# An attention and MoE kernel on one core: one weight quarter ahead of batch 1's tokens, and batch 1's transposes and state products moved in between the pieces of batch 0's second product

## The chip, the cores and the metric

The kernel runs on one core of one Trainium2 chip. The metric is the device time in microseconds (us), the median of three runs: 219.97 us before the change (219.83 to 220.05).

## The reference, cut to what matters

```python
# x: 8 batches, 8 heads, 512 tokens, 64;  state: 8, 8, 32, 64
scores  = x @ state^T / 8                 # softmax over the 32 states
xread   = softmax(scores)  @ state
scores2 = state @ x^T / 8                 # softmax over the 512 tokens
sread   = softmax(scores2) @ x
y = concatenate([xread, sread], axis=2)   # 544 rows per batch, 8 heads x 64 = 512 columns
h = y @ w_in                              # 512 x 2048
out = maximum(0.01 * h, h) @ w_out        # 2048 x 512
```

Inputs and output are fp32; the kernel computes in bf16 with fp32 sums.

## The kernel before, in words

**Algebra.** For the 512 token rows of a batch, xread @ w_in is never formed as such. The kernel multiplies the state by w_in first: M = state @ w_in, of 256 x 2048, held as two halves g of 128 rows (`a_m`, L322, in four column chunks c of 512; `m_evict`, L342, copies a chunk from PSUM to the tile M). FF1 is then `aT` (the probabilities, transposed) times M: per 128 columns j of the 2048, two matmuls (g = 0, 1) and one leaky relu on ACT into hT (`ff1`, L352; for batch 0 `ff1_0`, L570, and `relu0`, L577, two j at a time). FF2 is hT times w_out: for each of the four token tiles i, sixteen matmuls of 128 x 512, cut into four pieces jq of four matmuls (`piece`, L377). A piece with jq = 0 opens a PSUM bank for its tile, the one with jq = 3 copies it out and stores it. The state rows go through FF1 and FF2 at the end.

**Names used below.** PE is TensorE, DVE VectorE, ACT ScalarE, POOL GpSimd, SP SyncE. `VEC`, `SCA` and `POO` are copies on DVE, ACT and POOL. (b, c) behind M is batch and chunk. The softmax of a batch is `a_scores` (L209, PE, into the PSUM tile sc), `a_shift` (L260, DVE: row maxima mrow, spread mrowb, difference sh), `a_exp` (L264, ACT), `a_probs` (L267, DVE: sums, reciprocals, spread, product: aT). The second softmax is `a_max2` (L271, DVE, ends with mcols), `a_exp2` (L277, ACT, once per g, reads sc), `a_probs2` and `a_a2t` (DVE, and a transposed DMA on SP), and `a_sread` (PE).

**Order of work.** The schedule is manual: each engine runs its instructions in the order in which the code issues them, and waits in place for what an instruction needs. DMA queues too are in the order of issue: SP's, ACT's and POOL's. POOL issues all of w_in (four chunks), the tokens of batch 1, all of w_out (four quarters `load_w_out(c)`, c serves the pieces jq = c) and the tokens of batch 2. The tokens go to a buffer xl and are cast to bf16 (xb, `cast_x`, L102); batch 1's are transposed on PE (`a_xt_pe`, L190), 16 transposes in two PSUM banks, each copied to xT. The state of batches 2 to 7 is loaded by eight DMAs on SP (`load_state`, L162), cast by POOL and transposed by a DMA (`state_t`, L170): scores and M of batch 2 need it (st_t).

**PSUM.** There are eight banks: two of each of the tags ph and py, two in the one buffer "sc", two in the one buffer "big". A new tile of a tag waits until the last reader of the tile that had its bank is through.

**Around the change, before it.** Batch 0's tokens are cast in three steps (L518 to L522). Batch 0's FF1 (L584 to L605) ends with j = 14; in its loop, at j = 8, stand M(0,3), the scores of batch 0 and the cast of batch 1's tokens on DVE and POOL, and at j = 12 M(1,1). Then (L607 to L640) come exp2 of batch 0, the transposes of batch 1, pieces 0 and 1 of jq = 0, the scores of batch 1 with M(1,2), pieces 2 and 3 (in banks of ph), the loads of the state, exp and exp2 of batch 1, a_probs, the cast of batch 2's tokens on ACT, the pieces of jq = 1 and 2, jq = 3 for tiles 2 and 3, state_t. The loop at L648 is FF1 of batch 1 (s = 0 to 15), with the two last pieces of batch 0 and the first ones of batch 1 in between; at s = 2 are the transposes of batch 2, at s = 4 its scores, M(1,3) and M(2,0), at s = 8 its exp, at s = 10 and 11 its exp2, at s = 13 M(2,1) and M(2,2). The loop at L683 does batches 2 to 7.

Of the kernel before, what the change touches and what calls it, by code (L numbers as in the profile page):

```python
# [9 lines left out]
P = 128  # L10
B, H, S, D = 8, 8, 512, 64
NS = 32
DFF = 2048
DM = 512
SROW = S + NS
NT = S // P
# [4 lines left out]
FP32 = mybir.dt.float32  # L21
# [6 lines left out]
def kernel(  # L28
# [9 lines left out]
    nc = tc.nc  # L38
# [8 lines left out]
    psum = ctx.enter_context(tc.tile_pool(name="psum", bufs=2, space=bass.MemoryType.PSUM))  # L47
# [5 lines left out]
    VEC, SCA, POO = nc.vector.tensor_copy, nc.scalar.copy, nc.gpsimd.tensor_copy  # L53
# [38 lines left out]
    w_out_bf = wpool.tile([P, 16, DM], BF16, name="w_out_bf")  # L92
    xs, xl = {}, {}

    def load_x(b, eng):
        xl[b] = xpool.tile([P, H, NT * D], FP32, name="xl", tag="xl", bufs=2)
        eng.dma_start(xl[b][:], x[b].rearrange("h (p t) d -> p h (t d)", t=NT))

    def open_xb(b):
        xs[b] = xpool.tile([P, NT, H, D], BF16, name="xb", tag="xb")  # L100

    def cast_x(b, h0, h1, copy):  # L102
        copy(  # L103
            xs[b][:, :, h0:h1].rearrange("p t h d -> p h t d"),
            xl[b][:, h0:h1].rearrange("p h (t d) -> p h t d", t=NT),
        )

    def cast_x0(h0, h1, copy):
        u = h0 // NK
        copy(  # L110
            xs[0][:, :, h0:h1].rearrange("p t h d -> p h t d"),
            xf[u][:, h0 - NK * u:h1 - NK * u].rearrange("p h (t d) -> p h t d", t=NT),
        )

    def load_w_in(c):
        nc.gpsimd.dma_start(
            w_in_bf[:, :, DM * c:DM * (c + 1)],
            moe_w_in[:, DM * c:DM * (c + 1)].rearrange("(k p) f -> p k f", p=P),
        )

    def load_w_out(c):
        nc.gpsimd.dma_start(
            w_out_bf[:, 4 * c:4 * (c + 1), :],
            moe_w_out[DM * c:DM * (c + 1), :].rearrange("(j p) f -> p j f", p=P),
        )
# [33 lines left out]
    stf = consts.tile([P, B - 2, P], FP32, name="stf")  # L159
    stb = consts.tile([P, B - 2, P], BF16, name="stb")  # L160

    def load_state():  # L162
        for k in range(NK):
            for g in range(2):
                nc.sync.dma_start(
                    stf[NS * k:NS * (k + 1), :, D * g:D * (g + 1)],
                    state[2:, 2 * k + g].rearrange("b n d -> n b d"),
                )

    def state_t():  # L170
        POO(stb[:], stf[:])
        nc.sync.dma_start_transpose(st_t[:], stb[:].rearrange("p b q -> p (b q)"))
# [94 lines left out]
    def a_probs(a):  # L267
        a.aT = att.tile([P, 2, S], BF16, name="aT", tag="aT")
        block_probs(a.aT[:], a.e1, NB)
# [52 lines left out]
    def a_m(a, c, tag):  # L322
        if c == 0:
            a.M = mpool.tile([P, 2, DFF], BF16, name="M", tag="M")
        if tag in ("ph", "py", "phpy"):
            pm = [psum.tile([P, DM], FP32, name="pm", tag=t) for t in (tag[:2], tag[-2:])]
            at = [t[:] for t in pm]
        else:
            pm = psum.tile([P, 2, DM], FP32, name="pm", tag=tag, bufs=1)
            at = [pm[:, g, :] for g in range(2)]  # L330
        for k in range(NK):
            for g in range(2):
                v, r = (k // 2, 2 * (k % 2) + (g ^ (k // 2))) if a.b == 0 else (g, k)
                nc.tensor.matmul(  # L334
                    at[v][NS * r:NS * (r + 1)],
                    lhsT=st_of(a, g, k),
                    rhs=w_in_bf[D * g:D * (g + 1), k, DM * c:DM * (c + 1)],
                    start=True, stop=True,
                )
        return pm  # L340

    def m_evict(a, c, pm, copy):  # L342
        cols = slice(DM * c, DM * (c + 1))
        if isinstance(pm, list):
            for g in range(2):
                copy(a.M[:, g, cols], pm[g][:])  # L346
        else:
            copy(a.M[:, :, cols], pm[:])  # L348
# [25 lines left out]

    ys = {}

    def piece(b, hT, i, jq, tag="py", copy=SCA):  # L377
        if jq == 0:
            y = ys[b, i] = Y()
            y.py = psum.tile([P, DM], FP32, name="py", tag=tag)  # L380
        y = ys[b, i]
        for j in range(4 * jq, 4 * jq + 4):
            nc.tensor.matmul(  # L383
                y.py[:], lhsT=hT[:, j, P * i:P * (i + 1)], rhs=w_out_bf[:, j, :],
                start=(j == 0), stop=(j == 15),
            )
        if jq == 3:
            ysb = ypool.tile([P, DM], FP32, name="ysb", tag="ysb")
            copy(ysb[:], y.py[:])  # L389
            if b == B:  # L390
                for bb in range(4):
                    r0 = (4 * i + bb) * SROW + S
                    nc.sync.dma_start(out[r0:r0 + NS, :], ysb[NS * bb:NS * (bb + 1), :])
            else:
                nc.sync.dma_start(rows_of(b)[i], ysb[:])

    def rows_of(b):
        return out[b * SROW:b * SROW + S, :].rearrange("(p t) f -> t p f", t=NT)
# [20 lines left out]
    a0, a1, a2 = att_of[:3]  # L419
# [99 lines left out]
    cast_x0(2, 4, SCA)  # L519
    pxt = x0_half(0)  # L520
    xt0_evict(0, pxt, (VEC, SCA))
    cast_x0(4, 8, VEC)  # L522
    for c in range(2, 4):
        load_w_in(c)
    load_x(1, nc.gpsimd)
    for c in range(4):
        load_w_out(c)
    load_x(2, nc.gpsimd)
    a0.aT = att.tile([P, 2, S], BF16, name="aT", tag="aT")
# [18 lines left out]
    pm = a_m(a0, 0, "sc")  # L548
# [12 lines left out]
    h0 = hpool.tile([P, 16, S], BF16, name="hT", tag="hT")  # L561
# [5 lines left out]
        ph = [psum.tile([P, S], FP32, name="ph", tag=tag) for _ in range(2)]  # L567
        return ph, [p[:] for p in ph]

    def ff1_0(banks, j, g):  # L570
        for v in range(2):
            nc.tensor.matmul(  # L572
                banks[v], lhsT=a0.M[:, g, P * (j + v):P * (j + v + 1)], rhs=a0.aT[:, g, :],
                start=(g == 0), stop=(g == 1),
            )
# [7 lines left out]

    t0, b0 = open_ff1_0("py")  # L584
    t2, b2 = open_ff1_0("sc")
    for g in range(2):
        ff1_0(b0, 0, g)
        ff1_0(b2, 2, g)
    relu0(t0, 0)
    relu0(t2, 2)  # L590
    m_evict(a0, 2, a_m(a0, 2, "big"), VEC)
# [1 line left out]
    for j, tag in ((4, "py"), (6, "sc"), (8, "py"), (10, "ph"), (12, "py"), (14, "ph")):  # L593
        t, bk = open_ff1_0(tag)
        for g in range(2):
            ff1_0(bk, j, g)
        relu0(t, j)
        if j == 8:
            m_evict(a0, 3, a_m(a0, 3, "big"), VEC)
            a_scores(a0)  # L600
            a_max2(a0)
            cast_x(1, 0, 4, VEC)
            cast_x(1, 4, 8, POO)
        elif j == 12:
            m_evict(a1, 1, a_m(a1, 1, "big"), VEC)  # L605

    tags = ("py", "py", "ph", "ph")  # L607
    for g in range(2):
        a_exp2(a0, g)
    for t0 in (0, 2):  # L610
        ps = psum.tile([P, 2, NK, P], BF16, name="pxt2", tag="ph")
        a_xt_pe(a1, ps, t0, t0 + 2)
        VEC(a1.xT[:, t0:t0 + 2], ps[:])
    for i in (0, 1):
        piece(0, h0, i, 0, tags[i])
    a_scores(a1)
    m_evict(a1, 2, a_m(a1, 2, "big"), SCA)
    a_shift(a1)
    a_max2(a1)
    for i in (2, 3):  # L620
        piece(0, h0, i, 0, tags[i])
    nc.vector.memset(stf[:, 0, D - 1:D + 1], 0.0)
    load_state()
    a_exp(a1)
    for g in range(2):
        a_exp2(a1, g)
    a_probs(a1)
    open_xb(2)
    cast_x(2, 0, 8, SCA)
    for jq in (1, 2):  # L630
        for i in range(NT):
            piece(0, h0, i, jq, tags[i])
    for i in (2, 3):
        piece(0, h0, i, 3, tags[i], VEC if i % 2 else SCA)
    state_t()
    a_probs2(a0)
    a_a2t(a0)
    a_probs2(a1)
# [9 lines left out]
    for s in range(16):  # L648
        ff1(a1, h1, s)
        if s % 2:  # L650
            pb, hT, i, jq = fill[s // 2]
            piece(pb, hT, i, jq, copy=VEC if s == 3 else SCA)
        if s == 2:
            a_xt_full(a2)
            VEC(a2.xT[:], a2.pxt[:])
        elif s == 4:
            a_scores(a2)
            pm = a_m(a1, 3, "big"), a_m(a2, 0, "phpy")
            m_evict(a1, 3, pm[0], SCA)
            m_evict(a2, 0, pm[1], VEC)  # L660
            a_shift(a2)
            a_max2(a2)
            cast_x(3, 0, 8, POO)
        elif s == 8:
            a_exp(a2)
        elif s == 9:
            a_sread(a0)
        elif s in (10, 11):
            a_exp2(a2, s - 10)
            if s == 11:  # L670
                a_probs(a2)
                a_probs2(a2)
        elif s == 13:
            pm = [a_m(a2, 1, "big"), a_m(a2, 2, "sc")]
            m_evict(a2, 1, pm[0], VEC)
            m_evict(a2, 2, pm[1], SCA)
            a_open(att_of[3], 3)
            a_xt_dma(att_of[3])
# [4 lines left out]
    for b in range(2, B):  # L683
        hT = hpool.tile([P, 16, S], BF16, name="hT", tag="hT")
# [5 lines left out]
        for s in range(16):  # L690
# [38 lines left out]
            pb, i, jq = order[s]  # L729
# [6 lines left out]
    b = B - 1  # L736
# [43 lines left out]
```

## Time and profile before

| | |
|---|---|
| median of three runs | 219.97 us (219.83 to 220.05) |
| the profiled execution | 220.79 us |
| its span, first to last instruction | 218.7 us |
| PE busy | 210.1 us (96%) |
| ACT busy | 136.6 us (62%) |
| DVE busy | 102.9 us (47%) |
| POOL busy | 21.6 us (10%) |
| granted clock of PE | 1.00 |
| PE's share of the chain that ended last | 87% |

Times in the profile are microseconds from the start of the span. A row of the timeline gives start, duration, engine, line, operation, tiles and count, and in brackets the idle time of that engine just before, with what ended it. A row of the stretches gives the stretch, its length, and for PE, PE's weight loads, DVE, ACT and POOL the busy time with the number of instructions, then the granted clock, the DMA engines' share and GB/s. A matmul of 128 x 512 is shown as 0.379 us long, but the next one starts 0.216 us after it: matmuls overlap.

### The profile page before, as it was taken

To read this page: it belongs to the slowest core of one execution; us is meant where nothing else is said; L and a number is where in the kernel's file an instruction comes from. 1 tells how busy PE (TensorE), PEld (TensorE's weight loads), DVE (VectorE), ACT (ScalarE), POOL (GpSimd) and SP (SyncE) were. 2 spreads that over 40 slices of the span, in tenths; PEclk is the share of its full clock that TensorE was granted. 3 is DMA by queue.
4 is the path that set the end of the run, shared out by engine and by line. 5 is a ranking of instruction groups with operands and counts; after the bars stand their busy time and mean duration, and the time that the engine had idled before them with its cause. 6 is when DMAs were issued, how large, how long until landed. Compare 5 with 4: busy or idle time off the path is not lost.

```text
span 218.7 us, 3729 instructions
## 1 busy us (share of the span) xinstructions
PE 210.1 (96%) x1524; PEld 99.0 (45%) x1524; DVE 102.9 (47%) x155; ACT 136.6 (62%) x255; POOL 21.6 (10%) x35
## 2 busy tenths in 40 slices
PE   7999999996999999999999999999999999999994
PEld 2543444452345444444444444444444445466553
DVE  1768696699678408660767056724673000000000
ACT  3459646568869647964787477847685665554420
POOL 8811001003030003000300030000000000000000
PEclk9999999999999999999999999999999999999999
DMA  6999993986941493149313950271114111111123
GB/s 183 221 218 284 205 262 100 158 226 167 251 126 48 112 251 119 51 108 251 121 51 76 254 148 34 66 148 51 48 48 99 48 48 48 51 47 49 48 51 96
DMA packets 37632, 27.17 MB, mean 124 GB/s; under 512 B 22256, under 2 KB 32880, under 8 KB 37616
## 3 DMA queue, kind: packets, MB, share of 16 engines
q1 hardware_dynamic: 32704, 20.52, 36.0%
q0 software_dynamic: 4768, 6.29, 14.2%
q10 hardware_dynamic: 144, 0.13, 0.5%
q8 instruction: 12, 0.20, 0.4%
q14 instruction: 4, 0.03, 0.1%
HBM read 17.30 MB, written 8.91 MB: 120 GB/s over the span
## 4 chain that ended last, share of the span: by engine, by line
PE 87%; DVE 5%; DMA 3%; ACT 2%; SPq 1%; issue 1%; ACTq 0%
PE py L383 50%; PE ph L355 20%; PE pm L334 4%; PE ph L366 3%; PE pspin L130 2%; PE ph L572 2%; DMA st_t<-stb 2%; PE psr L307 1%; PE sc L213 1%; DVE mcols L275 1%; PE php L572 1%; DMA out_dram<-ysb 1%; DVE M L346 1%; DVE mrowb L231 1%; DVE M L348 1%; DVE sh L233 1%
## 5 line engine op out<-in xcount | busy, mean ns | idle before, releaser
L383 PE MATMUL py<-w_out_bf,hT 128*128 128x512 bf16 x496 | 125.5, 379 | 0.0
L360 ACT ACTIVATE hT<-ph 128x512 bf16<-128x512 f32 x112 | 67.0, 601 | 42.6 <-PE ph L355 42.6
L383 PEld LDWEIGHTS <-hT 128*128 128x128 bf16 x496 | 47.0, 98 | 57.4 <-issue 4.9
L355 PE MATMUL ph<-aT,M 128*128 128x512 bf16 x224 | 66.1, 379 | 2.2 <-ACT hT L360 1.9
L355 PEld LDWEIGHTS <-M 128*128 128x128 bf16 x224 | 21.6, 98 | 29.1 <-issue 3.9
L389 ACT COPY ysb<-py 128x512 f32<-128x512 f32 x31 | 18.2, 586 | 11.5 <-PE py L383 11.5
L223 DVE TRANSPOSE_TENSOR_REDUCE mrow<-sc 128x32 f32<-128x1024 f32 x7 | 8.7, 1249 | 32.1 <-PE sc L213 32.1
L411 DVE COPY ysh<-pyh 128x256 f32<-128x256 f32 x1 | 0.4, 425 | 47.7 <-PE pyh L406 47.7
L103 POOL CAST xb<-xl 128x2048 bf16<-128x2048 f32 (+1 forms) x6 | 10.5, 1751 | 89.1 <-DMA xl<-in_x_dram 69.9
L348 ACT CAST M<-pm 128x1024 bf16<-128x1024 f32 x14 | 14.2, 1013 | 3.3 <-PE pm L334 2.9
L245 DVE TRANSPOSE_TENSOR_REDUCE r<-e 128x32 f32<-128x1024 bf16 x7 | 8.7, 1242 | 9.6 <-ACT e L240 9.6
L348 DVE CAST M<-pm 128x1024 bf16<-128x1024 f32 x10 | 12.2, 1218 | 1.6 <-PE pm L334 1.6
L346 DVE CAST M<-pm 128x512 bf16<-128x512 f32 x14 | 9.0, 685 | 7.4 <-PE pm L334 7.4
L281 ACT ACTIVATE e<-sc,mcols 128x512 bf16<-128x512 f32 x16 | 11.1, 699 | 0.9 <-DVE mcols L275 0.6
L273 DVE TENSOR_REDUCE mcol<-sc 128x2 f32<-128x1024 f32 x8 | 9.7, 1214 | 0.0
L240 ACT ACTIVATE e<-sh 128x1024 bf16<-128x1024 f32 x7 | 7.4, 1051 | 3.5 <-DVE sh L233 3.5
L370 ACT ACTIVATE hs<-ph 128x256 bf16<-128x256 f32 x16 | 6.0, 385 | 4.6 <-PE ph L366 4.4
L231 DVE STREAM_TRANSPOSE mrowb<-mrow 128x1024 f32<-128x1024 f32 x7 | 8.7, 1245 | 0.2
L254 DVE STREAM_TRANSPOSE qb<-qh 128x1024 bf16<-128x1024 bf16 x7 | 8.7, 1245 | 0.2
L233 DVE TENSOR_TENSOR sh<-sc,mrowb 128x1024 f32<-128x1024 f32 x7 | 8.6, 1224 | 0.2
L366 PE MATMUL ph<-sr_t,w_in_bf 128*128 128x256 bf16 x64 | 8.3, 273 | 0.0
L580 ACT ACTIVATE hT<-ph 128x512 bf16<-128x512 f32 x12 | 6.5, 595 | 2.3 <-PE ph L572 2.3
(93 smaller groups left out, 147.3 us busy)
## 6 DMA issues: line engine op xcount, KB each, us to landing
out_dram<-ysb SPq DMA_DIRECT2D x31, 256.0 KB, 2.3
xl<-in_x_dram SPq DMA_DIRECT2D x5, 1024.0 KB, 6.7
w_in_bf<-in_moe_w_in_dram POOLq DMA_DIRECT2D x4, 512.0 KB, 9.3
xl<-in_x_dram POOLq DMA_DIRECT2D x2, 1024.0 KB, 18.0
w_out_bf<-in_moe_w_out_dram POOLq DMA_DIRECT2D x4, 512.0 KB, 18.5
xf<-in_x_dram SPq DMA_DIRECT2D x2, 512.0 KB, 5.0
out_dram<-ysb SPq DMA_DIRECT2D x8, 64.0 KB, 1.7
stf<-in_state_dram SPq DMA_DIRECT2D x8, 48.0 KB, 2.0
```

What stands on the lines that cost most here:

```text
L103: copy(xs[b][:, :, h0:h1].rearrange("p t h d -> p h t d"), xl[b][:, h0:h1].rearrange("p h (t d) -> p h t d", t=NT),)
L231: nc.vector.transpose(m1b[:], m1[:, :, None].to_broadcast([P, n, NS]))
L233: nc.vector.tensor_tensor(out=sh[:], in0=flat, in1=m1b[:].rearrange("p c j -> p (c j)"), op=ALU.subtract,)
L273: nc.vector.tensor_reduce(out=m2[:], in_=a.sc[:], axis=AX.X, op=ALU.max, negate=True)
L281: nc.scalar.activation(out=a.e2[:, g], in_=a.sc[:, g, :], func=AF.Exp, bias=a.m2s[:, g:g + 1], scale=SCALE, accum_out=a.r2[:, g:g + 1],)
L346: copy(a.M[:, g, cols], pm[g][:])
L348: copy(a.M[:, :, cols], pm[:])
L355: nc.tensor.matmul(ph[:], lhsT=a.M[:, g, P * j:P * (j + 1)], rhs=a.aT[:, g, :], start=(g == 0), stop=(g == 1),)
L360: nc.scalar.activation(out=hT[:, j, :], in_=ph[:], func=AF.Prelu, alpha=0.01)
L366: nc.tensor.matmul(ph[:, :n], lhsT=w_in_bf[:, k, P * j:P * (j + 1)], rhs=sr_t[:, k, :], start=(k == 0), stop=(k == NK - 1),)
L383: nc.tensor.matmul(y.py[:], lhsT=hT[:, j, P * i:P * (i + 1)], rhs=w_out_bf[:, j, :], start=(j == 0), stop=(j == 15),)
L389: copy(ysb[:], y.py[:])
```

## The change

Nothing is computed that was not computed before. What moves:

- **Loads.** The first quarter of w_out is queued ahead of batch 1's tokens. Heads 6 and 7 of batch 0's tokens are cast on POOL, ahead of that in POOL's order, instead of on DVE.
- **Batch 0's FF1.** The eight matmuls of j = 0 to 3 come in another order. The cast of batch 1's tokens moves behind the loop and is split three ways: heads 0 to 3 on DVE, 4 and 5 on ACT, 6 and 7 on POOL. M(1,1) leaves the loop.
- **Batch 0's FF2.** Pieces 2 and 3 use a two-bank tile in "big" instead of banks of ph. Three pieces of jq = 0 go ahead of batch 1's transposes, the fourth behind them. The second half of the transposes is copied by ACT instead of DVE. The loads of the state are issued behind those copies, ahead of the scores of batch 1.
- **Batch 1's M.** Chunks 1, 2 and 3 are multiplied in banks of ph, behind the scores and behind pieces 1 and 3 of jq = 1, and copied by ACT, all ahead of a_exp of batch 1. Before, chunk 1 was in FF1 of batch 0 and copied by DVE, chunk 3 in FF1 of batch 1.
- **Behind it.** state_t is issued ahead of the pieces of jq = 2. Both of the pieces 2 and 3 are copied out by DVE. M(2,0) is multiplied in "big" and copied by ACT, where it was in ph and py and copied by DVE.

```diff
-    def piece(b, hT, i, jq, tag="py", copy=SCA):
+    def piece(b, hT, i, jq, bank=None, copy=SCA):
         if jq == 0:
             y = ys[b, i] = Y()
-            y.py = psum.tile([P, DM], FP32, name="py", tag=tag)
+            y.py = psum.tile([P, DM], FP32, name="py", tag="py")[:] if bank is None else bank
...
-    cast_x0(4, 8, VEC)
+    cast_x0(4, 6, VEC)
     for c in range(2, 4):
         load_w_in(c)
+    cast_x0(6, 8, POO)
+    load_w_out(0)
     load_x(1, nc.gpsimd)
-    for c in range(4):
+    for c in range(1, 4):
         load_w_out(c)
     load_x(2, nc.gpsimd)
...
-    for g in range(2):
-        ff1_0(b0, 0, g)
-        ff1_0(b2, 2, g)
+    ff1_0(b0, 0, 0)
+    ff1_0(b2, 2, 0, (0,))
+    ff1_0(b0, 0, 1)
+    ff1_0(b2, 2, 0, (1,))
+    ff1_0(b2, 2, 1)
...
             a_max2(a0)
-            cast_x(1, 0, 4, VEC)
-            cast_x(1, 4, 8, POO)
-        elif j == 12:
-            m_evict(a1, 1, a_m(a1, 1, "big"), VEC)
-
-    tags = ("py", "py", "ph", "ph")
+    cast_x(1, 0, 4, VEC)
+    cast_x(1, 4, 6, SCA)
+    cast_x(1, 6, 8, POO)
+
     for g in range(2):
         a_exp2(a0, g)
-    for t0 in (0, 2):
+    for i in (0, 1):
+        piece(0, h0, i, 0)
+    wide = psum.tile([P, 2, DM], FP32, name="pyw", tag="big", bufs=1)
+    piece(0, h0, 2, 0, bank=wide[:, 0])
+    for t0, copy in ((0, VEC), (2, SCA)):
         ps = psum.tile([P, 2, NK, P], BF16, name="pxt2", tag="ph")
         a_xt_pe(a1, ps, t0, t0 + 2)
-        VEC(a1.xT[:, t0:t0 + 2], ps[:])
-    for i in (0, 1):
-        piece(0, h0, i, 0, tags[i])
+        copy(a1.xT[:, t0:t0 + 2], ps[:])
+    piece(0, h0, 3, 0, bank=wide[:, 1])
+    nc.vector.memset(stf[:, 0, D - 1:D + 1], 0.0)
+    load_state()
     a_scores(a1)
-    m_evict(a1, 2, a_m(a1, 2, "big"), SCA)
+    m_evict(a1, 1, a_m(a1, 1, "ph"), SCA)
     a_shift(a1)
     a_max2(a1)
-    for i in (2, 3):
-        piece(0, h0, i, 0, tags[i])
-    nc.vector.memset(stf[:, 0, D - 1:D + 1], 0.0)
-    load_state()
+    for i in range(NT):
+        piece(0, h0, i, 1)
+        if i in (1, 3):
+            c = 2 + i // 2
+            m_evict(a1, c, a_m(a1, c, "ph"), SCA)
     a_exp(a1)
     for g in range(2):
         a_exp2(a1, g)
     a_probs(a1)
+    state_t()
     open_xb(2)
     cast_x(2, 0, 8, SCA)
-    for jq in (1, 2):
-        for i in range(NT):
-            piece(0, h0, i, jq, tags[i])
+    for i in range(NT):
+        piece(0, h0, i, 2)
     for i in (2, 3):
-        piece(0, h0, i, 3, tags[i], VEC if i % 2 else SCA)
-    state_t()
+        piece(0, h0, i, 3, copy=VEC)
...
         elif s == 4:
             a_scores(a2)
-            pm = a_m(a1, 3, "big"), a_m(a2, 0, "phpy")
-            m_evict(a1, 3, pm[0], SCA)
-            m_evict(a2, 0, pm[1], VEC)
+            m_evict(a2, 0, a_m(a2, 0, "big"), SCA)
```

## The prediction, made before the changed kernel was run

> **What bounds the kernel now.** I read the page's first lines and the busy times by stretch, then TensorE's (PE) rows with the wait ahead of each, and last the rows of ACT, DVE and POOL around each wait.
>
> ```profile
> PE 210.1 (96%) x1524; PEld 99.0 (45%) x1524; DVE 102.9 (47%) x155; ACT 136.6 (62%) x255; POOL 21.6 (10%) x35
> ...
> 20.00:57.00 37.00, 33.77 (x243) 15.15 (x241) 30.71 (x46) 24.35 (x45) 3.76 (x3) 1.00 0.87 186
> 57.00:95.00 38.00, 38.00 (x271) 17.19 (x277) 22.34 (x32) 27.71 (x54) 3.79 (x2) 1.00 0.50 128
> 95.00:205.00 110.00, 110.00 (x719) 51.94 (x704) 38.47 (x54) 71.18 (x135) 3.79 (x2) 1.00 0.33 90
> ```
>
> Second number of a stretch: PE's busy time. From 57 to 205 us PE never stops, at a granted clock of 1.00. The change removes no matmul, so it can only win back PE's waits before 57 us. These are the rows of PE that waited:
>
> ```profile
> 23.37 1.09 PE L193 MATMUL pxt<-ident,xb 128*128 128x128 bf16 x16 [0.47 <-ACT hT L580]
> ...
> 37.99 0.59 PE L355 MATMUL ph<-aT,M 128*128 128x512 bf16 x2 [0.35 <-DVE ysb L389]
> ...
> 42.94 0.41 PE L213 MATMUL sc<-xT,st_t 64*32 64x512 bf16 x8 [0.45 <-DMA st_t<-stb]
> ...
> 50.46 0.59 PE L355 MATMUL ph<-aT,M 128*128 128x512 bf16 x2 [0.92 <-ACT hT L360]
> ...
> 53.32 0.59 PE L355 MATMUL ph<-aT,M 128*128 128x512 bf16 x2 [0.98 <-ACT hT L360]
> ```
>
> The brackets understate the loss, because a matmul's modelled end lies about 0.16 us after the next could start. By start-to-start steps (0.216 between 128x512 matmuls, 0.309 into or out of a group of quarter-array matmuls) they cost 0.63, 0.51, 0.51, 1.08 and 1.14. With 0.23 at 20.55 (j = 12 waits for DVE's M copy), 4.10 us is lost from 20 us on; that is the most there is to win.
>
> **The change, by time.**
>
> *Prelude (to 20 us): nothing.* cast_x0(6,8) goes from DVE to POOL. xf[1] lands near 6.7 (issued 1.25, about 5.4 to landing). POOL casts 128x1024 in 1.04 and 128x2048 in 1.89, so 128x512 in about 0.61, done near 7.4; PE transposes those heads at 8.1. That 0.7 hides it; without the cover it costs at most its 0.61. In ff1_0's new order bank 0 closes one matmul earlier (0.216), so the relus start near 14.70 instead of 14.92, but the chain passes through PE and DVE's M copy (19.27 to 20.49): 0.04 at most.
>
> *Queue order.* POOL's queue lands in issue order: w_in at 9.1 to 17.7, xl of batch 1 at 20.5, w_out at 23.6, 25.4, 27.9 and 30.8, xl of batch 2 at 33.7 (issue plus time to landing). With w_out 0 moved ahead, it lands near 20.5 and batch 1's tokens take the place at 23.4 to 23.6; what follows keeps its place.
>
> *22 to 27 us.* M(1,1) leaves the loop (0.43), so j = 14 ends at 22.24 and its relus at 23.42. PE goes on with three pieces, 12 x 0.216: to 24.83. Meanwhile the tokens are cast, from 23.45: 0.69 on DVE and 0.62 on ACT (their rows of the same shapes), 0.61 on POOL.
>
> The trace shows that DVE and POOL can exclude each other:
>
> ```profile
> 49.99 1.89 POOL L103 CAST xb<-xl 128x2048 bf16<-128x2048 f32 x1 [11.91 <-DMA xl<-in_x_dram]
> ...
> 50.00 1.91 DVE L275 TENSOR_SCALAR mcols<-mcol 128x2 f32<-128x2 f32 x1
> ```
>
> The DVE row is normally 0.17; here it lasts as long as POOL's cast. I therefore put POOL's cast behind DVE's: 23.45 + 0.69 + 0.61 = 24.75, just under 24.83. Side by side they would end at 24.15, still under the pieces, so the sum is the same.
>
> The Trainium skill, "SBUF — State Buffer", section "Who interferes with whom", says that a DVE copy, cast or tensor_scalar in a two-port mode and a GpSimd instruction lock each other out for a whole instruction. It speaks against splitting one landing's cast over these two engines; by it the casts end at 24.75, by free overlap at 24.15.
>
> The first half's transposes run from 24.85 (8 in 0.48); DVE copies it 25.5 to 26.2 and ACT the second half 25.94 to 26.95 (as 1.01 for 128x1024), after exp2 of batch 0 (24.0 to 25.5). Piece 3 covers PE to 26.65; scores(1) would go at 26.75 and goes at 27.05: **0.3 lost**, in place of 0.63.
>
> *27 to 38 us.* Scores with M(1,1): next piece at 27.6. Two pieces, M(1,2) (0.43), two pieces, M(1,3) (0.43): 31.93, where before two M groups were paired with others. A lone group costs PE 0.43, a second one beside it 0.22 more (steps of the trace); there is one more switch in and out, **0.2 lost**. From 31.93 PE has jq = 2 of four pieces and jq = 3 of two: 6 x 4 x 0.216 = 5.18, to 37.12. Batch 1's softmax (aT) must be ready by then. Before, it was:
>
> ```profile
> 30.42 1.06 ACT L240 ACTIVATE e<-sh 128x1024 bf16<-128x1024 f32 x1 [2.59 <-DVE sh L233]
> ...
> 31.64 1.24 DVE L245 TRANSPOSE_TENSOR_REDUCE r<-e 128x32 f32<-128x1024 bf16 x1
> ...
> 34.80 0.69 DVE L255 TENSOR_TENSOR aT<-e,qb 128x1024 bf16<-128x1024 bf16 x1
> ```
>
> aT was ready at 35.49 and PE came at 37.05. Now three M copies (each 2 x 0.5 on ACT) stand ahead of this exp in ACT's queue, and the third can't begin before M(1,3) is multiplied: group at 31.59, copy 32.05 to 33.12, exp 33.05 to 34.1. DVE's sh is ready at 31.3 and waits. From exp's end DVE needs 3.85 (31.64 to 35.49): aT at 37.98, first ff1 of batch 1 at 38.05. **0.93 lost**: a new wait. Behind exp on ACT stand exp2 (to 35.45) and the cast of batch 2 (to 37.35), both done before the first relu at 38.65.
>
> *State.* load_state's eight issues (0.44 each) begin when DVE's memset is through, 26.3 instead of 31.7; they share the DMA engines with w_out 2, 3 and batch 2's tokens, so I let them land between 32 and 35 (2.0 after the last issue, to that plus a 3 us share of the busy queue). Cast 0.83, transposed DMA 4.5: st_t by 38 to 41; needed at 42.9. The 0.51 wait goes. The delay of w_out 2 and 3 is covered by 3 to 4 us.
>
> *38 us on.* Pieces 2 and 3 no longer hold ph, so 37.99's 0.51 goes. PE from 38.05: four ff1 pairs (0.43 each) and two pieces with the 16 transposes (0.89) reach scores(2) at 42.9, as before, and with M(1,3) done earlier s = 5 starts at 43.48 instead of 43.72. M(2,0) moves from DVE to ACT, so mrow starts at 43.4, not 45.05; sh is ready at 47.2, not 48.83. ACT reaches exp(2) at 47.6: relu 9 ends at 49.15 (ff1 11 waits **0.1**), relu 11 stands behind exp2 and ends at 51.37 (ff1 13 waits **0.47**). Instead of 2.22. The probabilities of batch 2 are ready by 53.4, PE wants them at 55.1.
>
> *Sum.* Left or new: 0.23 + 0.3 + 0.2 + 0.93 + 0.1 + 0.47 = 2.23, instead of 4.10: 1.9 less. ff1 13 starts at 51.42 instead of 53.32, and from there PE has no wait. Span 218.7 - 1.9 = 216.8. The profiled execution took 220.79, 2.1 beyond its span and 0.8 above the median 219.97; taken off the median: **218.1**.
>
> **Rivals.**
>
> *A. POOL holds DVE again.* xl of batch 3 is issued behind two transposed DMAs on SP, near 42.8, and lands 6.1 later: POOL's 1.89 starts at 48.9. DVE's mcols comes at 48.35. If it is 0.6 later, it waits until 50.85, exp2 starts 0.7 late, and relu 11 with it. The same with the state's cast (0.83) inside aT's chain. For it: the row at 50.00. Against: 0.6 of room. It gives 218.8.
>
> *B. More than that.* If ACT's rows pack closer, or the copy of M(1,3) starts sooner, the 0.93 and the 0.47 shrink: 217.0 (216.7 without either).
>
> *C. The new wait eats it.* Every step to aT is now in series with PE's order. Tokens 0.5 late, state's cast in the chain (0.83) and A (0.7) leave the gain near nothing: 219.5 to 220.4, the same.
>
> *D. Slower.* One mechanism: batch 1's tokens land later than the pieces cover. Its place is PE's first transpose, its price one for one from casts ending at 24.83, that is, from landing at 23.5. The gain is gone at 25.4, and beyond 25.85 it is slower. Landing together with w_out 2 (27.9), where packets of the transfers mix, would cost 27.9 - 23.5 = 4.4: 222.5. For it: the queue is full without a break until 34, and landing lags the bytes. Against: all seven transfers landed in issue order.
>
> **How the numbers follow.** The forecast has 0.55 (its own range 217.3 to 218.6), A 0.15, B 0.08, C 0.09, D 0.13. Faster by over 0.2% (0.44 us, about what a measurement of this kernel can tell) are the first three: 0.78; same 0.09; slower 0.13. The range 216.9 to 219.7 leaves out D, half of C and a little of B.
>
> **What would show it.** Right: no wait of PE near 23, transposes at 24.9, a wait of about 0.9 for DVE's aT ahead of ff1 near 38, none for st_t, mrow right behind scores(2), one wait of about 0.5 near 51. Wrong: batch 1's tokens landing after 24; a wait of PE for POOL's cast; aT later than 38.3; mcols again near 1.9 us long; w_out waits in the pieces.

## The result

The change was forecast to be 0.9% faster (218.1 us). Its first four executions have a median of 221.96 us (221.66 to 222.29) against 219.97: ratio 1.0091, 95% interval [1.0074, 1.0109], slower. Measured again later (run e12 below) it has 220.40 against 220.15: 1.0027 [1.0004, 1.0050]. A ratio here is an estimate from the executions and need not be the quotient of the two medians. The executions of the change fall into two groups, near 220.3 and near 222.0, and both are above the forecast range of 216.9 to 219.7.

The profiled execution took 222.05 us, its span is 220.2 (before: 218.7). PE's busy time by stretch, in the columns explained above:

```profile
20.00:57.00 37.00, 33.63 (x234) 14.83 (x235) 26.75 (x40) 25.25 (x48) 3.85 (x3) 0.95 0.84 189
57.00:95.00 38.00, 38.00 (x265) 17.29 (x264) 22.43 (x32) 28.13 (x54) 3.79 (x2) 1.00 0.51 130
95.00:205.00 110.00, 110.00 (x717) 51.51 (x715) 39.22 (x57) 71.14 (x134) 3.79 (x2) 1.00 0.33 89
```

Behind 57 us PE is busy without a break, as before and as forecast. From 20 to 57 PE idles as long as before (3.37 us, 3.23 before), and the granted clock is 0.95. The waits of PE in that stretch, and the rows behind the long one:

```profile
26.70 0.41 PE L213 MATMUL sc<-xT,st 64*32 64x512 bf16 x8 [0.24 <-ACT xT L619]
...
33.34 2.75 PE L383 MATMUL pyw<-w_out_bf,hT 128*128 128x512 bf16 x12
38.86 1.24 PE L383 MATMUL pyw<-w_out_bf,hT 128*128 128x512 bf16 x4 [2.77 <-DVE ysb L389]
39.90 1.92 PE L355 MATMUL ph<-aT,M 128*128 128x512 bf16 x4
41.60 1.69 PE L383 MATMUL py<-w_out_bf,hT 128*128 128x512 bf16 x4
43.13 0.59 PE L355 MATMUL ph<-aT,M 128*128 128x512 bf16 x2
...
54.79 0.59 PE L355 MATMUL ph<-aT,M 128*128 128x512 bf16 x2 [0.30 <-ACT hT L360]
```

Of the five waits shown before, four are gone or below 0.1, and the last is down from 0.98 to 0.30. The new one at 26.70 was forecast. But another new one stands at 38.86, where none was expected: inside FF2 of batch 0, at the last piece (jq = 3) of tile 3. By start-to-start steps it costs 3.145 - 0.216 = 2.93. Behind it four matmuls take 1.92 and 1.69 us instead of 1.03: half clock. The clock became whole at 5.40, fell to half at 39.53 and was whole again at 42.95. The stretches, with the last 3.41 us ahead of the fall by themselves (the clock stands behind the five engines):

```profile
5.40:36.12 30.72, 29.43 (x328) 13.26 (x327) 20.64 (x35) 21.61 (x40) 7.42 (x9) 1.00 1.14 225
36.12:39.53 3.41, 0.67 (x4) 0.31 (x4) 2.65 (x3) 1.05 (x1) 0.83 (x1) 1.00 0.16 33
39.53:42.95 3.42, 3.42 (x10) 1.22 (x9) 2.40 (x9) 1.19 (x2) 0.00 (x0) 0.50 0.56 181
```

From the matmul at 39.51 to the one at 43.13 PE does nine steps in 3.63 us that take 1.94 at full clock: 1.69 lost. What PE waits for at 38.86 is DVE's copy, which stands behind DVE's product aT; the third row is POOL's cast, which runs beside that product:

```profile
36.96 1.25 DVE L255 TENSOR_TENSOR aT<-e,qb 128x1024 bf16<-128x1024 bf16 x1
38.13 0.68 DVE L389 COPY ysb<-pyw 128x512 f32<-128x512 f32 x1
...
36.84 0.83 POOL L171 CAST stb<-stf 128x768 bf16<-128x768 f32 x1 [12.19 <-DMA stf<-in_state_dram]
```

DVE copies tile 2 out of the first bank of pyw at 38.13, as soon as batch 1's aT is through, and only then PE begins tile 3 in the other bank. Tiles 2 and 3 share no bank, but they share one PSUM tile (`wide`, two banks). In the profile the first matmul of tile 3's last piece waits for DVE, and no other matmul of the two tiles does. The kernel before has these two tiles in PSUM tiles of their own, and there 48 matmuls of FF2 run on, tile 3's last piece among them, while tile 2 is only being copied out:

```profile
26.68 10.53 PE L383 MATMUL py<-w_out_bf,hT 128*128 128x512 bf16 x48
...
36.38 0.59 ACT L389 COPY ysb<-py 128x512 f32<-128x512 f32 x1 [0.83 <-PE py L383]
```

**Theory.** A write into one bank of the two-bank tile waits for the last reader of the other bank. The reader is tile 2's copy, which stands on DVE behind batch 1's whole softmax; the wait of 2.9 that this makes also halves PE's clock for 3.4 us. **Rival.** The chain to aT is the bound, and the wait between the pieces only shows it in another place.

### The profile page after: what moved, and what is told of

Its sections match the earlier page's. It is cut to its first block, busy times and chain, and to the rows that moved or that the text cites. A ratio compares the mean times of both kernels' runs of the same rounds, so it can differ in the third digit from the quotient of the medians.

```text
span 220.2 us, 3735 instructions
## 1 busy us (share of the span) xinstructions
PE 211.4 (96%) x1524; PEld 98.9 (45%) x1524; DVE 100.2 (45%) x152; ACT 139.3 (63%) x261; POOL 22.3 (10%) x36
## 4 chain that ended last, share of the span: by engine, by line
PE 78%; DMA 10%; ACT 4%; SPq 2%; DVE 2%; POOL 1%; issue 1%; ACTq 0%; POOLq 0%
PE py L383 46%; PE ph L355 22%; DMA xl<-in_x_dram 7%; PE pm L334 3%; PE ph L366 3%; DMA xf<-in_x_dram 3%; SPq L393 2%; PE psr L307 1%; PE pyw L383 1%; PE sc L213 1%; ACT hT L360 1%; ACT e L240 1%; PE pxt L193 1%; DMA out_dram<-ysb 1%; DVE qb L254 1%; DVE r L245 1%
## 5 line engine op out<-in xcount | busy, mean ns | idle before, releaser
L383 PE MATMUL py<-w_out_bf,hT 128*128 128x512 bf16 x464 | 119.4, 381 | 0.0
L355 PE MATMUL ph<-aT,M 128*128 128x512 bf16 x224 | 66.8, 384 | 0.3 <-ACT hT L360 0.3
L389 ACT COPY ysb<-py 128x512 f32<-128x512 f32 x30 | 17.6, 586 | 11.2 <-PE py L383 11.2
L348 ACT CAST M<-pm 128x1024 bf16<-128x1024 f32 x13 | 13.2, 1013 | 1.1 <-PE pm L334 0.6
L348 DVE CAST M<-pm 128x1024 bf16<-128x1024 f32 x9 | 10.9, 1217 | 1.5 <-PE pm L334 1.5
L383 PE MATMUL pyw<-w_out_bf,hT 128*128 128x512 bf16 x32 | 8.0, 386 | 2.8 <-DVE ysb L389 2.8
L346 DVE CAST M<-pm 128x512 bf16<-128x512 f32 x12 | 7.7, 685 | 6.3 <-PE pm L334 6.3
```

The source lines that it names most:

```text
L355: nc.tensor.matmul(ph[:], lhsT=a.M[:, g, P * j:P * (j + 1)], rhs=a.aT[:, g, :], start=(g == 0), stop=(g == 1),)
L383: nc.tensor.matmul(y.py, lhsT=hT[:, j, P * i:P * (i + 1)], rhs=w_out_bf[:, j, :], start=(j == 0), stop=(j == 15),)
L389: copy(ysb[:], y.py)
```

## The experiments

Medians of several executions stand against runs of the kernel before on the same chip (220.03 to 220.15); e13 to e16 are single executions. A wait "by steps" is the time from one matmul's start to the next one's, less the usual step (0.216 between matmuls of 128x512).

**e1: both pieces, then both copies**

```diff
-    for i in (2, 3):
-        piece(0, h0, i, 3, copy=VEC)
+    for part in ((True, False), (False, True)):
+        for i in (2, 3):
+            piece(0, h0, i, 3, copy=VEC, part=part)
```

> The change with one edit: the last pieces (jq = 3) of tiles 2 and 3 are multiplied one behind the other, and the two copies follow. Nothing is left out. Theory (a wait that the two-bank tile makes: PE's first matmul into the second bank waits until DVE has copied the first bank, which stands in DVE's order behind batch 1's probabilities; the 2.93 us of it then halve PE's clock for 3.4 us): no wait between the pieces, ff1 of batch 1 waits for aT instead, to about 38.2 in the change's times where it began at 39.90 (1.65 won), and at full clock (1.5 more): 221.96 - 3.2 = 218.8. Rival (the chain to aT bounds it and the pieces only hide that): the same wait moves to ff1 and still halves the clock; at most the 1.65 is won: 220.3 or more.

Measured 219.23 (218.51 to 219.99), ratio 0.9960 [0.9942, 0.9977]. Waits of PE in its profile:

```profile
38.45 1.04 PE L355 MATMUL ph<-aT,M 128*128 128x512 bf16 x4 [1.21 <-DVE aT L255]
...
58.24 0.41 PE L213 MATMUL sc<-xT,st_t 64*32 64x512 bf16 x8 [0.82 <-DMA xT<-xb]
```

The wait between the pieces is gone with this edit alone, the clock is whole in all twelve executions, and the kernel is now faster than before. The profile is of the slowest of them (219.99). FF1 of batch 1 begins at 38.45, after a wait of 1.37 for aT: the forecast's new wait, there. The second row, batch 3's scores waiting for their transposed DMA, no theory had.

**e2: tile 2 copied by ACT** (`copy=VEC if i % 2 else SCA`)

> The change with one edit: tile 2 is copied out by ACT, tile 3 by DVE. Nothing is left out. Theory: the wait between the pieces stays but ends with ACT's copy, which stands behind its cast of batch 2 (ends 37.2): copy to 37.8, piece at 37.9 instead of 38.86 (1.0 won), and the wait of 1.9 is too short to halve the clock (1.7 more): 221.96 - 2.7 = 219.3. If 1.9 still halves the clock: 221.0. Rival (aT bounds): no change in where ff1 begins, 221.9.

Measured 219.30 (219.07 to 220.03), 0.9968 [0.9956, 0.9979]. Tile 3's piece begins right behind ACT's copy (37.05 to 37.63), while DVE is still at aT (37.08 to 38.18):

```profile
37.68 1.02 PE L383 MATMUL pyw<-w_out_bf,hT 128*128 128x512 bf16 x4 [1.68 <-ACT ysb L389]
```

Whoever makes the copy ends the wait, and the wait is not for aT. The clock is whole in all twelve.

**e3: eight idle matmuls in the wait** (`spin(8, "ph")` between the two pieces)

> The change with eight idle matmuls of 128x512 into a free PSUM bank between the last pieces of tiles 2 and 3: extra work that nothing uses, 8 x 0.216 = 1.73 us inside the 2.93 us wait. Theory: the wait ends at the same time for DVE's copy, but the clock stays whole: 221.96 - 1.7 = 220.3. Rival (the half clock has another reason, such as a phase of its own): half clock as before and 222.0.

Measured 220.25 (220.06 to 220.98), 1.0013 [1.0003, 1.0023]:

```profile
36.32 1.89 PE L130 MATMUL pspin<-idle 128*128 128x512 bf16 x8
38.70 1.02 PE L383 MATMUL pyw<-w_out_bf,hT 128*128 128x512 bf16 x4 [0.49 <-DVE ysb L389]
39.56 1.03 PE L355 MATMUL ph<-aT,M 128*128 128x512 bf16 x4
```

The wait ends where it did (38.70), and four matmuls take 1.03 again. The profile alone shows little, since this wait was shorter anyway (2.38 without the idle matmuls, as aT took 0.69 instead of 1.25). The executions show it: all twelve have the whole clock (0.998 to 1.00 over the span), where ten of eighteen of the change have the half clock (0.991 to 0.992; the first four, five of e12, and e13). With the idle matmuls the kernel takes what the quick group of the change takes. The half clock is the idle stretch's doing.

**e4: batch 0's split cast alone, in the kernel before**

> The kernel before, with only batch 0's cast split: heads 4 and 5 on DVE, 6 and 7 on POOL behind the loads of w_in. Nothing is left out. In the profile of the change batch 0's FF1 began at 13.09, before it at 13.63. Theory (the split is free but wins nothing, since PE isn't waiting for these heads; the 0.54 is where PE's clock became whole, 5.40 instead of 7.16): 220.0, the same. Rival (the split wins the 0.54): 219.4.

Measured 220.26, 1.0007 [0.9997, 1.0017]: nothing won. In its profile batch 0's FF1 begins at 13.11, but so it does in e6, which has no split (13.15), while e1, which has it, begins at 13.60. The 0.5 comes and goes in the prelude; in these three profiles the clock became whole at 6.11, 4.43 and 6.22, in the one of before at 7.16. What moves it isn't settled.

**e6: queue order alone, in the kernel before**

> The kernel before, with only the queue order changed: the first quarter of w_out ahead of batch 1's tokens. Nothing is left out. Theory (the order alone costs; the transposes had to move with it): tokens land at 23.5 instead of 20.5, DVE's and POOL's casts end one behind the other near 25.2, PE's transposes begin there instead of at 23.37: +1.9, 221.9; 1.7 more if the wait of 2.7 halves the clock. Rival (the tokens have room anyway): 220.0.

Measured 222.40 (221.51 to 224.09), 1.0110 [1.0078, 1.0143], and its profile has a stretch of half clock behind the waits of 1.52 and 0.77 at the transposes. Two of the six executions have that half clock (223.15 and 224.09); the others took 221.51 to 222.51. Expected were 221.9, and 1.7 more with half clock. The order of the queue costs about what it was priced at, unless the transposes move with it.

**e8: three idle matmuls**

> The change with three idle matmuls instead of eight between the last pieces of tiles 2 and 3: 0.65 of the wait filled, 2.3 left idle. Nothing uses them. Theory (an idle stretch of 1.9 keeps the clock whole, one of 2.9 halves it): between them, so this tells where; 220.3 if 2.3 keeps it whole, 222.0 if not. Rival (clock has a reason of its own): 222.0 and the half clock at another place.

Measured 220.33, with one of ten executions at 221.97. That one has the half clock (0.992). In the profile only 1.73 us of the wait stay idle, so it does not test the 2.3 that it was meant for; the clock is whole.

**e5: exp of batch 1 ahead of the copy of M(1,3)**, on top of e1

```diff
+            if i == 3:
+                a_exp(a1)
             m_evict(a1, c, a_m(a1, c, "ph"), SCA)
-    a_exp(a1)
```

> As the kernel with both last pieces ahead of the copies, and batch 1's exp stands on ACT ahead of the copy of M(1,3) instead of behind it. Nothing is left out. Theory (what is left then is aT's chain behind ACT's M copies): exp starts when DVE's sh is ready, near 31.0 instead of 32.7, aT is ready near 36.0 ahead of POOL's cast of the state, so ff1 of batch 1 has no wait (1.4 won against the kernel without this edit); the scores of batch 2 then come near 41.7 and wait for the state's transposed DMA (lands near 42.2), which gives back 0.5: 218.8 - 0.9 = 217.9. Rival (ACT's order is free, aT is bound by DVE alone): 218.8 as without it.

Measured 218.90, 0.9949 [0.9933, 0.9965]. FF1 of batch 1 begins without a wait, so the 1.4 in front of it is won, as expected:

```profile
36.88 1.03 PE L355 MATMUL ph<-aT,M 128*128 128x512 bf16 x4
```

The state isn't waited for. But batch 3's scores wait 1.29 at 57.06 for their transposed DMA, so only 0.3 of it reaches the end. The 217.9 expected had no such wait. Three of the next runs (e7, e9, e11) move one DMA, batch 3's tokens, on SP.

**e7: batch 3's tokens right behind the state's loads**

> As the kernel with exp ahead, and the load of batch 3's tokens is issued on SP right behind the state's loads, ahead of the state's transposed DMA, instead of behind those of batch 0's and 1's second probabilities. Nothing is left out. Theory (with the pieces' wait gone, what ends last is batch 3's chain of load, POOL's cast and transposed DMA, for which its scores waited 1.29 in the profile of the kernel with exp ahead): no wait there, 218.9 - 1.3 = 217.6. Rival (the load only collides with the state's loads and batch 2's tokens, and PE waits for the state instead): 218.9 or more.

Measured 218.80, 0.9947 [0.9934, 0.9960]. No wait at batch 3; instead DVE and then PE:

```profile
39.53 1.86 DVE L287 TENSOR_SCALAR r<-r 128x2 f32<-128x2 f32 x1
...
39.45 1.91 POOL L103 CAST xb<-xl 128x2048 bf16<-128x2048 f32 x1 [1.47 <-DMA xl<-in_x_dram]
...
43.42 0.41 PE L213 MATMUL sc<-xT,st_t 64*32 64x512 bf16 x8 [1.29 <-DVE xT L664]
```

The tokens land at 39.4, POOL casts them at once, an operation of 0.16 on DVE takes 1.86, and batch 2's xT behind it is late. The gain went into a new wait of the same size.

**e9: behind the state's transposed DMA**

> As the kernel with exp ahead; the load of batch 3's tokens is issued on SP right behind the state's transposed DMA, between the two places tried so far. Nothing is left out. Theory (both places cost PE 1.29: issued at 33.5, the tokens land at 39.4 and POOL's cast holds DVE's small operation for 1.86, so batch 2's xT is late; issued at 43.2 they land at 49.5 and batch 3's own transposes are late): issued near 38.8 they land near 45, POOL's cast runs beside operations of DVE that it doesn't hold, and neither wait is left: 218.9 - 1.3 = 217.6. Rival (one of the two waits is there for another reason): 218.8.

Measured 218.57, 0.9928 [0.9910, 0.9946]. Neither wait is left, but a third one came:

```profile
40.91 5.95 SPq L299 DMA_TRANSPOSE a2T<-a  x2
...
48.55 0.64 PE L307 MATMUL psr<-a2T,xb 128*128 128x64 bf16 x16 [1.10 <-DMA a2T<-a]
```

The two transposed DMAs stand behind the 1 MB load on SP. SP takes 5.95 to issue them instead of 2.61 in the change, and they land 6.9 after their issue (median) instead of 3.3.

**e10: e9 with each copy behind its piece again**

> As the kernel with batch 3's tokens behind the state's DMA, but with each copy behind its piece again, as in the change. Nothing is left out. Theory (the second bank always waits for the first bank's copy, and what that costs is set by where the copy stands in DVE's order): aT is through at 36.1 here, so the copy goes at once, 36.15 to 36.85, and the piece begins at 36.9 instead of 35.95: one wait of 0.95, 217.6 + 0.95 = 218.5, clock whole. Rival (the wait in the change is for aT itself): 217.6.

Measured 218.70, 0.9940 [0.9918, 0.9962]:

```profile
35.39 0.69 DVE L255 TENSOR_TENSOR aT<-e,qb 128x1024 bf16<-128x1024 bf16 x1
36.16 0.69 DVE L389 COPY ysb<-pyw 128x512 f32<-128x512 f32 x1
...
36.91 1.02 PE L383 MATMUL pyw<-w_out_bf,hT 128*128 128x512 bf16 x4 [0.78 <-DVE ysb L389]
```

The piece starts at 36.91 and the wait by steps is 0.95, both as expected: the wait is there with aT done 0.8 earlier, and its price is the copy's place on DVE. The end moved by 0.13 only, because the wait for a2T shrank at the same time, in brackets from 1.10 to 0.28.

**e11: between the two transposed DMAs**

> As the kernel with exp ahead; the load of batch 3's tokens is issued on SP between the two transposed DMAs of the second probabilities of batch 0 and of batch 1. Nothing is left out. Theory (SP's queue is in order, so whoever stands behind the 1 MB load lands late: with the load ahead of both, PE waited 1.19 for batch 0's): issued near 41.5 the load lands near 47.7, batch 0's probabilities land before it, batch 3's transposes near 54, needed at 55.8; none of the three waits is left: 218.57 - 1.1 = 217.5. Rival (the transposed DMAs wait for the engines, not for the queue): 218.6.

Measured 218.85 (217.74 to 219.08), 0.9921 [0.9898, 0.9944]; the profiled execution took 217.76, and PE idles 0.65 in it between 20 and 57 us. **e15** and **e16** are two more executions of it:

> The kernel with batch 3's load between the two transposed DMAs, one look: 217.75 as in its profile, with no wait of PE but those of 0.2 to 0.3; or 218.9 as in four of its six executions, and then the profile shows which wait holds the 1.1. Theory: batch 3's load lands later in those, and its transposes are waited for. Rival: PE's clock becomes whole later in the prelude (0.5 of it).

> The same kernel, a second look: 217.75 without such a wait, or 218.9 with the one that holds the 1.1.

They took 218.59 and 218.56. In both, batch 3's scores wait for the transposed DMA again (e15):

```profile
56.83 0.41 PE L213 MATMUL sc<-xT,st_t 64*32 64x512 bf16 x8 [0.86 <-DMA xT<-xb]
```

So the theory has the right wait and the wrong link: the tokens land as early as in the quick execution (POOL's cast at 48.51 and 48.65, there 48.44), it is the transposed DMA that takes 6.2 from issue to landing instead of 4.8. Why it does isn't settled.

**e12: the change again**

> The change as it is, beside the other. Theory: the wait of 2.9 between the last pieces of tiles 2 and 3 and half a clock for 3.4 us behind it are there in every execution: 222.0, of narrow spread. Rival (the half clock comes and goes with a phase of its own): runs near 220.3 among them.

Measured 220.40: seven executions at 220.07 to 220.48, five at 221.72 to 222.35. Over the span the seven have a granted clock of 0.999 to 1.00, the five 0.992, as the first four had (0.991 to 0.992): the groups are those without and with the half clock. The expected narrow spread is wrong, the rival's line is what came. **e13** and **e14**, one execution each, ask for the reason:

> The change as it is, one look. In the profiles so far the clock changes only at steps of 3.413 us from the moment at which it became whole (5.40 and 39.53 in the change's profile, ten steps apart). Theory (a step in which PE idles about 2.0 us or more is followed by a step at half clock; where the wait of 2.7 to 2.9 is cut by the border of two steps into parts below that, the clock stays whole): about 222.0 with one part of the wait over 2.0 inside one step, or about 220.3 with both below. Rival (length of the wait alone): half clock always, or a wait that is shorter in the quick executions.

> The change as it is, a second look, as the first: 222.0 with over 2.0 us of the wait inside one step of 3.413 us, or 220.3 with the wait cut by a border.

They took 221.63 and 220.54, one of each group. PE's busy time in the clock's 3.413 us steps, counted from where it became whole, with PE's weight load of tile 2's last matmul and the piece behind the wait, e13:

```profile
35.69 0.10 PEld L383 LDWEIGHTS <-hT 128*128 128x128 bf16 x1
...
38.40 1.39 PE L383 MATMUL pyw<-w_out_bf,hT 128*128 128x512 bf16 x4 [2.54 <-DVE ysb L389]
...
35.51:38.92 3.41, 0.87 (x5) 0.45 (x5) 2.76 (x4) 1.35 (x1) 0.83 (x1) 1.00 0.12 24
38.92:42.33 3.41, 3.41 (x10) 1.22 (x9) 2.37 (x9) 1.19 (x2) 0.00 (x0) 0.50 0.61 188
```

and e14:

```profile
36.16 0.10 PEld L383 LDWEIGHTS <-hT 128*128 128x128 bf16 x1
...
38.92 1.02 PE L383 MATMUL pyw<-w_out_bf,hT 128*128 128x512 bf16 x4 [2.60 <-DVE ysb L389]
...
34.97:38.39 3.42, 1.35 (x7) 0.59 (x6) 3.28 (x6) 2.35 (x3) 0.83 (x1) 1.00 0.01 3
38.39:41.80 3.41, 2.88 (x14) 1.34 (x14) 2.19 (x8) 1.18 (x3) 0.00 (x0) 1.00 0.58 160
```

In both profiles the record of tile 2's last matmul is missing: eleven matmuls are shown where the kernel has twelve, but the weight load of the twelfth is there. Counted with it, PE waits 2.49 in e13 and 2.54 in e14, and the steps that hold the wait have 0.22 more of busy time than their rows say, 1.09 and 1.57. So e14's wait is the longer of the two, and yet its clock stays whole: a border at 38.39 cuts it. The length alone doesn't decide. Where PE was busy for 0.67, 1.08 or 1.09 of 3.41 (the change, e12, e13) the next step was at half clock; with 1.57 (e14) or 1.85 (e8, with the same record missing) it wasn't. e6 lies between, and was followed by half clock:

```profile
21.50:24.91 3.41, 1.44 (x10) 0.54 (x10) 1.83 (x2) 2.96 (x8) 1.48 (x1) 1.00 1.22 204
24.91:28.32 3.41, 3.41 (x20) 2.01 (x18) 1.38 (x2) 0.00 (x0) 0.00 (x0) 0.50 1.24 207
```

In idle time, 1.97 (e6) halved the clock and 1.84 (e14) didn't, so the limit of about 2.0 fits. It rests on the nearest profile on each side and on modelled ends of matmuls, and part of e6's busy time is transposes.

The Trainium skill, "TensorE: Matmul & The Clock Gate", section "What's actually happening", gives a free-running window of 3413 ns and half rate after at least one idle window. The length agrees with the steps here (3.413); "idle" is not to be read as empty, since windows in which PE was busy for 1.09 (e13) and 1.44 (e6) of 3.41 were enough.

## Why the prediction was wrong, step by step

- **The step that failed** is the one from 31.93 to 37.12 us: "jq = 2 of four pieces and jq = 3 of two: 6 x 4 x 0.216 = 5.18". It has six groups in a row and no wait among them. Each piece's needs were checked for hT, w_out and its bank, but not for the other half of its PSUM tile, and the change's note that both copies go to DVE was read as work for DVE, not as something that PE waits for behind aT. e1, e2 and e10 show the wait to be for the copy, at the copy's place, and not for aT. Against the forecast, FF1 of batch 1 began at 39.90 instead of 38.05: 1.85. Of it 0.23 is aT itself (38.21 instead of 37.98), the rest is the copy and tile 3's piece, which stand behind aT now.
- **What the wait does to the clock** was no term at all: 1.69, of which 1.51 fell behind 39.90. 1.85 + 1.51 = 3.36 is the whole of 220.2 - 216.8. It comes and goes with the phase of the clock's steps, about 1.55 between the two groups of e12. In time the miss is larger, 221.96 - 218.1 = 3.9: the forecast took 0.8 off, because the profiled execution before lay that far above its median, and the change's profiled execution (222.05) lies only 0.1 above its own.
- **No case was that.** Rival D had the slower side, by tokens landing late. They landed at 23.5, as forecast, and PE had no wait ahead of its transposes. Inside them it waited 0.2 for POOL's cast near 24.6, which the prediction lists as a sign of being wrong; PE had come 0.55 earlier than forecast, by the prelude below.
- **What held:** casts end at 24.64 (24.75 forecast; POOL's 128x512 took 1.13 beside DVE's 0.69, so one cast behind the other fits better than side by side, 24.15); scores of batch 1 wait 0.31 (0.3); exp stands behind three M copies; no wait for the state; ff1 11 and 13 wait 0.09 and 0.46 (0.1 and 0.47); batch 2's mrow right behind its scores. The 0.93 ahead of FF1 of batch 1 was right in kind, 1.37 in e1. Rival A's mcols was held again, 1.05 long at 51.71, and cost PE nothing beyond the forecast there.
- **Why 1.37:** the state landed at 36.8, not between 32 and 35, and POOL's cast fell on the last operation of aT's chain, 1.15 long in e1 (1.25 in the change) instead of 0.69. That was named in rivals A and C, with 0.83.
- **The 0.54 of the prelude** in the profile (FF1 of batch 0 at 13.09) is no part of the change (e4, e6).
- **What the forecast would still have missed:** e1, which lacks the false wait, has 219.23 and not 218.1: beside the larger wait for aT, batch 3's transposed DMA is the next thing that is late. The prediction has no term for it ("from there PE has no wait"). Its chain in e1 is the load at 43.4, landing at 50.1, the cast, and 6.1 for the transposed DMA, which took 4.3 before.

So the change without the wait that the shared tile makes is faster than before by 0.4% (e1), and with exp ahead and batch 3's load moved by 0.7 to 0.8% (e9, e11).

## What to carry to other kernels

Read every wait in the new instruction order, and ask of each who stands ahead of the one it names; two halves of one tile can wait for each other though they share no bank, so put all the writes ahead of the reads (e1), or give them tiles of their own, as the kernel before had (not tried in the changed kernel). An idle stretch of PE of 2.5 us or more cost more than its length here in some executions and not in others: measure such a kernel often, and look for two groups. When a bound is lifted, the next is often one transfer away: here one load had three places, and each place made another engine wait.

## What the runs showed of the hardware

- **A load beside another, busy queue can start late.** The state's eight loads were issued from 25.93 on in the change and took 8.0 us (median) to land, against 2.0 before, where POOL's queue had nearly drained; their first packets moved near 29, three microseconds after the issue, while POOL's queue was at work.
- **POOL holds DVE beyond copies.** The product that makes aT, with two inputs in SBUF, took 1.10 to 1.25 instead of 0.69 where POOL's cast ran beside it (the change, e1, e2), and 0.69 where the cast was about over (e3). The Trainium skill, "SBUF — State Buffer", section "Who interferes with whom", says that such an operation contends with a GpSimd operation that reads SBUF; these rows agree.
- **A transposed DMA of 128x2048** took 4.3 to 6.2 from issue to landing in these profiles, with nothing changed in it.
